# A constant column as second source for a clamp and a normalisation, and a scalar operand for a minimum

## The chip, the core and the metric

The kernel runs on one core of one Trainium2 chip. The metric is the device time of one execution in microseconds (us). The core has five engines that run side by side and wait for one another through semaphores: TensorE (PE, with its weight loads shown apart as PEld), VectorE (DVE), ScalarE (ACT), GpSimd (POOL) and SyncE (SP), which issues all DMAs here. A profiled execution gives the busy time of each engine, every instruction's start and duration, and the clock that TensorE was granted, as a share of full speed.

## The reference

Block attention over 8 batches, 8 heads, 576 positions and head width 64 is followed by a feed-forward layer over the 8 x 576 = 4608 tokens:

```
scores = scale * q @ k.T                     # masked where block_i < block_j, blocks of 64
attn   = exp(scores - rowmax);  attn /= rowsum + 1e-9
x      = heads of (attn @ v), side by side   # 4608 x 512
h      = x @ w_in                            # 512 x 2048
g      = h if h >= 1, 0 if h <= -1, else (h + 1)^2 / 4
out    = g @ w_out                           # 2048 x 512
```

Everything is fp32 in memory.

## The kernel before, in words

TensorE multiplies in a reduced-precision fp32 form (F32R). So an operand that needs full precision is split into a high part, which is the value cast to that form, and a low part, which is the remainder, and a product is three matmuls: high by high, high by low, low by high.

**Attention** goes over 32 pairs (`Pair`): 8 batches by 4 pairs of heads. For each pair, `scores` makes tiles of scores in PSUM for one head (two matmuls, L484 and L487), DVE takes the row maxima (L508), ACT exponentiates and adds up the rows (L513), DVE adds a small constant (L494), takes reciprocals (L495) and multiplies the tile by them (L519). The last 64 query rows of both heads are handled together by `scores_last`: it is 576 columns wide, in two halves, so it has two maxima (L533), the smaller of their negatives is taken (L537), ACT exponentiates (L539), and DVE makes the reciprocal of the sum (L543, L547) and multiplies the 128x576 tile `pr` by it in place (L548). TensorE then transposes the normalised tiles (L561 in batch 0, L559 later), they are copied out, and multiplied with v (L598). Batches 0 and 1 are "plain" (`PLAIN = 2`): the normalised weights and v are used there as plain fp32, without the split. There are 4 pairs in a batch, so 8 of the 32 pairs are plain.

**The weights** are converted once, at the start. `convert` handles a piece of 128x512 words, of which there are 16 of `w_in` and 16 of `w_out`: a DMA brings the words, ACT scales them in two steps (L170, L171), DVE clamps the scaled value between two constants (L172), shifts it (L175) and joins the sign bit to it (L178), POOL adds the low part (L184), ACT casts the high part (L186) and POOL subtracts to get the low part (L188). The high and low parts of `w_in` stay in SBUF (`wih`, `wil`), and those of `w_out` go back to memory (`wo_split`). The words lie in `bits`, a pool of three buffers, so a piece can only be loaded when the piece three before it is finished. L172 and L175 read one operand from SBUF, and L178 reads two.

**The feed-forward layer** goes in 9 chunks of 512 tokens by 16 column blocks of 128. `ffn_in` makes `ph` with twelve matmuls (L777) and the gate from it (ACT L786, DVE L787 and L790, ACT L791, POOL L792), and `ffn_out` multiplies by `w_out` (L801, L806).

**Order.** The loop at the bottom of the kernel walks through the steps of attention, eight a pair. Before step 36 it also draws 12 weight pieces (and two more ahead), after it one feed-forward step for each step of attention, and the remaining pieces as the feed-forward layer needs them. When attention is done, the remaining feed-forward steps follow. The source sets dependencies and priorities; a scheduler then lays out each engine's instructions as one fixed list when the program is built, by its own estimates of how long each takes. An engine runs its list strictly in that order. A changed instruction can therefore change the order of others.

Of the kernel before, what the change touches and what calls it, by code (L numbers as in the profile page):

```python
# [8 lines left out]
F32 = mybir.dt.float32  # L9
F32R = mybir.dt.float32r  # L10
AF = mybir.ActivationFunctionType
ALU = mybir.AluOpType
# [11 lines left out]
def block_attn_then_ffn(  # L24
# [9 lines left out]
    nc = tc.nc  # L34
    B, H, S, D = q.shape
    NT, DM = out.shape
    DF = w_in.shape[1]
    P = 128
# [16 lines left out]
    CW = 512  # L55
    F32_TOP = float.fromhex("0x1.dffffcp-96")
# [7 lines left out]
    const = ctx.enter_context(tc.tile_pool(name="const", bufs=1))  # L64
# [13 lines left out]
    def work_bank(name):  # L78

        banks["n"] += 1  # L80
        if banks["free"] and banks["n"] % 2:
            return ps_o.tile([P, 512], F32, tag="po", name=name)
        return ps_w.tile([P, 512], F32, tag="work", name=name)
# [23 lines left out]
    def last_blocks(t_):  # L107
# [19 lines left out]
        out=msel[:NTL, : NTL * BLK].rearrange("p (t c) -> p t c", c=BLK),  # L127
# [24 lines left out]


    shifted = []

    def wide_tile(dtype, name):
        return conv.tile([P, 2 * CW], dtype, tag="bits", name=name)

    def convert(n, source, hi, lo, done):

        bits = wide_tile(I32, "bits").rearrange("p (n t) -> p n t", t=2)
        if not shifted:
            shifted.append(att1.tile([P, CW], U32, tag="x32", name="shifted"))
        tmp = shifted[0]
        nc.sync.dma_start(bits, source.bitcast(I32).rearrange("p (n t) -> p n t", t=2))
        top, low = bits[:, :, 1].bitcast(F32), bits[:, :, 0]
        words = top.bitcast(U32)


        nc.scalar.mul(top, top, 2.0**-112)  # L170
        nc.scalar.mul(low, low.bitcast(U32), 2.0**-29)  # L171
        nc.vector.tensor_scalar(  # L172
            out=top, in0=top, scalar1=F32_TOP, scalar2=-F32_TOP, op0=ALU.min, op1=ALU.max
        )
        nc.vector.tensor_scalar(  # L175
            out=tmp, in0=words, scalar1=3, scalar2=None, op0=ALU.logical_shift_left
        )
        nc.vector.scalar_tensor_tensor(  # L178
            out=words, in0=words, scalar=0x80000000, in1=tmp,
            op0=ALU.bitwise_and, op1=ALU.bitwise_or,  # L180
        )
        yield
        w32 = bits[:, :, 1]
        nc.gpsimd.tensor_tensor(out=w32, in0=w32, in1=low, op=ALU.add)  # L184
        w32 = w32.bitcast(F32)
        nc.scalar.copy(hi(), w32)  # L186
        yield
        nc.gpsimd.tensor_tensor(out=lo(), in0=w32, in1=hi().bitcast(F32), op=ALU.subtract)  # L188
        if done:
            done()  # L190
# [26 lines left out]
    def prepare_weights():  # L217

        live = []
        for n, piece in enumerate(weight_pieces()):  # L220
            live = [c for c in live + [convert(n, *piece)] if next(c, True) is None]
            yield
        for _ in range(LAG):
            live = [c for c in live if next(c, True) is None]
            yield
# [8 lines left out]
    def as_float32r(src, plain):  # L234

        if plain:
            wide = src.shape[1] > RING - 2 * S
            places = SPARE_WIDE if wide else SPARE
            moved = [places[spare[wide] % len(places)]]
            spare[wide] += 1  # L240
            if src.shape[1] > TCH:
                if "end" not in spare:
                    spare["end"] = att1.tile([P, G0 + P], F32R, tag="pa11", name="pre")[:, :BLK]
                moved.append(spare["end"])
            for i, dst in enumerate(moved):
                n = min(TCH, src.shape[1] - i * TCH)
                nc.sync.dma_start(dst[:, :n].bitcast(F32), src[:, i * TCH : i * TCH + n])
            return moved
        n, moved = src.shape[1], []
        wide = wide_tile(F32R, "prr")  # L250
        nc.sync.dma_start(wide[:, :n].bitcast(F32), src)
        for c0 in range(0, n, TCH):
            moved.append(wide[:, c0 : min(c0 + TCH, n)])
        return moved


    class Pair:
# [264 lines left out]
        def scores_last(self):  # L522

            half = S // 2
            pr = att3.tile([P, S], F32, tag="pr", name="pr")
            nm = small.tile([P, 3], F32, tag="nm", name="nm")
            sm = small.tile([P, 3], F32, tag="sm", name="sm")
            banks = []
            for i in range(2):
                ps = work_bank("ps_s")  # L530
                for j in range(2):
                    self.product(ps[:, :half], j, SM, i * half, half, j == 0, j == 1)
                nc.vector.tensor_reduce(  # L533
                    out=nm[:, i : i + 1], in_=ps[:, :half], axis=AX.X, op=ALU.max, negate=True
                )
                banks.append(ps)
            nc.vector.tensor_tensor(out=nm[:, 2:3], in0=nm[:, 0:1], in1=nm[:, 1:2], op=ALU.min)  # L537
            for i in range(2):
                nc.scalar.activation(  # L539
                    pr[:, i * half : (i + 1) * half], banks[i][:, :half], AF.Exp,  # L540
                    bias=nm[:, 2:3], scale=1.0, accum_out=sm[:, i : i + 1],
                )
            nc.vector.tensor_scalar(  # L543
                out=sm[:, 2:3], in0=sm[:, 0:1], scalar1=sm[:, 1:2], scalar2=EPS,
                op0=ALU.add, op1=ALU.add,
            )
            nc.vector.reciprocal(sm[:, 2:3], sm[:, 2:3])  # L547
            nc.vector.tensor_scalar_mul(pr, pr, sm[:, 2:3])  # L548
            self.pr["last"] = as_float32r(pr, self.plain) if self.hop else [pr]

        def split(self, ps, hi, lo=None):
# [340 lines left out]
```

## Time and profile before

| | us |
|---|---|
| median of 3 runs | 1239.24 (1237.13 to 1243.8) |
| the profiled execution, its time | 1239.06 |
| its span, first to last instruction | 1237.3 |
| PE busy | 1186.6 (96%) |
| DVE busy | 863.8 (70%) |
| ACT busy | 698.5 (56%) |
| POOL busy | 371.8 (30%) |

The time of the profiled execution is 1.8 us more than its span, which is what lies around the first and the last instruction. A row of the groups of instructions reads: line, engine and operation, output and input tile, shape, count, then the busy time of the group and the mean duration of one in ns, then the idle time of the engine just before them and what ended it. A row of the chain of waits reads: start in us, length in us, what held the chain there. A row of a table by stretches gives, for each stretch, its length, the busy time of each engine with its number of instructions, the granted TensorE clock, the busy share of the DMA engines and the memory traffic.

### The profile page before, as it was taken

Reading aid. Unit: us, or ns where it says so; the run is one execution under the profiler, and the core shown is the slowest. Engines: PE = TensorE matmul, PEld = TensorE weight load, DVE = VectorE, ACT = ScalarE, POOL = GpSimd, SP = SyncE. Lnnn points to the kernel's source line nnn. Section 1 sums busy time; section 2 is a strip of 40 time slices with the busy share of each in tenths; the row PEclk is TensorE's granted clock in tenths of the full one; section 3 lists DMA queues with packets and bytes.
Section 4 is the critical chain, followed back from the end, with each engine's and each line's share of the span. In section 5 each row is a group of like instructions: output and inputs, shape, how many; then the busy total and the mean of one; then the engine's idle time right before and its main releaser. Section 6 shows DMA issues by size and latency. Waiting matters only on the chain.

```text
span 1237.3 us, 19822 instructions
## 1 busy us (share of the span) xinstructions
PE 1186.6 (96%) x6280; PEld 993.1 (80%) x6280; DVE 863.8 (70%) x2124; ACT 698.5 (56%) x1731; POOL 371.8 (30%) x366
## 2 busy tenths in 40 slices
PE   4878898999999999999999999999999999999998
PEld 3666677788888888888888888888888888888886
DVE  8888778658777877787777877787778776322322
ACT  5877667546566656665666665666566654222222
POOL 3444546312222222222222222222222222222222
PEclk9988998999999999999999999999999999999999
DMA  5756776778986655565555555565556443333332
GB/s 165 213 176 208 235 247 221 225 202 255 291 270 219 192 162 156 147 198 166 163 159 180 164 160 160 148 196 151 155 149 192 142 135 111 119 102 102 120 103 102
DMA packets 177192, 215.40 MB, mean 174 GB/s; under 512 B 109872, under 2 KB 128304, under 8 KB 176320
## 3 DMA queue, kind: packets, MB, share of 16 engines
q1 hardware_dynamic: 177088, 214.14, 56.1%
q8 instruction: 50, 0.82, 0.3%
q14 instruction: 54, 0.44, 0.1%
HBM read 134.74 MB, written 31.98 MB: 135 GB/s over the span
## 4 chain that ended last, share of the span: by engine, by line
PE 86%; DVE 5%; DMA 4%; ACT 2%; issue 2%; POOL 1%; SPq 0%; ACTq 0%; DVEq 0%; POOLq 0%
PE ph L777 31%; PE po L801 20%; PE po L806 10%; PE ps_av L598 9%; PE ps_s L484 5%; PE ps_s L487 4%; PE ps_t L559 4%; PE ps_qk L403 1%; DMA bits<-in_moe_w_in_dram 1%; DVE bits L172 1%; POOL bits L184 1%; PE ps_t L561 1%; DVE nm L508 1%; DVE bits L178 1%; DVE shifted L175 1%
## 5 line engine op out<-in xcount | busy, mean ns | idle before, releaser
L792 POOL TENSOR_TENSOR gl<-t,gh 128x512 fp32r<-128x512 f32 x144 | 186.5, 1295 | 522.8 <-ACT gh L791 338.2
L801 PE MATMUL po<-wo,gh 128*128 128x512 f32 x1152 | 294.1, 396 | 0.1
L801 PEld LDWEIGHTS po<-wo,gh 128*128 128x128 f32 x1152 | 211.2, 188 | 43.3 <-ACT gh L791 0.6
L777 PE MATMUL ph<-xh,wih 128*128 128x512 f32 x576 | 232.7, 404 | 0.4 <-DVE t L790 0.4
L777 PE MATMUL ph<-xh,wil 128*128 128x512 f32 x576 | 228.1, 396 | 0.0
L777 PE MATMUL ph<-xl,wih 128*128 128x512 f32 x576 | 226.9, 394 | 0.0
L787 DVE SCALAR_TENSOR_TENSOR t<-t 128x512 f32<-128x512 f32 x144 | 101.0, 701 | 161.5 <-ACT t L786 158.6
L786 ACT ACTIVATE t<-ph 128x512 f32<-128x512 f32 x144 | 86.2, 599 | 160.5 <-PE ph L777 160.5
L791 ACT CAST gh<-t 128x512 fp32r<-128x512 f32 x144 | 89.4, 621 | 118.9 <-DVE t L790 118.8
L806 PE MATMUL po<-wo,gl 128*128 128x512 f32 x576 | 155.3, 391 | 0.0
L484 PE MATMUL ps_s<-ka,qa 68*128 68x288 f32 (+4 forms) x384 | 133.8, 363 | 4.9 <-DMA ka<-mrow 4.0
L513 ACT ACTIVATE pr<-ps_s,nm 128x128 f32<-128x128 f32 x192 | 100.4, 525 | 57.5 <-DVE nm L508 56.4
L508 DVE TENSOR_REDUCE nm<-ps_s 128x1 f32<-128x128 f32 (+3 forms) x256 | 118.9, 482 | 16.4 <-PE ps_s L487 15.6
L777 PEld LDWEIGHTS ph<-xh,wil 128*128 128x128 f32 x576 | 109.1, 189 | 24.0
L806 PEld LDWEIGHTS po<-wo,gl 128*128 128x128 f32 x576 | 108.0, 188 | 22.9
L777 PEld LDWEIGHTS ph<-xl,wih 128*128 128x128 f32 x576 | 109.6, 190 | 19.3
L777 PEld LDWEIGHTS ph<-xh,wih 128*128 128x128 f32 x576 | 109.2, 190 | 19.3 <-DVE t L790 0.8
L381 POOL TENSOR_TENSOR vsr<-vn,vsr 64x64 fp32r<-64x64 f32 (+1 forms) x96 | 56.5, 589 | 227.1 <-ACT vsr L380 226.0
L487 PE MATMUL ps_s<-kb,qb 128*128 128x288 f32 (+4 forms) x384 | 120.4, 321 | 0.0
L790 DVE TENSOR_TENSOR t<-ph,t 128x512 f32<-128x512 f32 x144 | 98.7, 685 | 2.0
L559 PEld LDWEIGHTS ps_t<-ident_r,prr 128*128 128x128 f32 x600 | 68.5, 139 | 22.4 <-issue 0.5
L494 DVE TENSOR_SCALAR sm<-sm 128x1 f32<-128x1 f32 x256 | 38.5, 151 | 65.0 <-ACT pr L513 54.8
(115 smaller groups left out, 1879.7 us busy)
## 6 DMA issues: line engine op xcount, KB each, us to landing
wo<-wo_split SPq DMA_DIRECT2D x144, 512.0 KB, 3.4
prr<-pr SPq DMA_DIRECT2D x96, 192.0 KB, 3.0
prr<-pr SPq DMA_DIRECT2D x48, 256.0 KB, 2.8
out_dram<-ob SPq DMA_DIRECT2D x36, 256.0 KB, 2.9
bits<-in_moe_w_in_dram SPq DMA_DIRECT2D x16, 512.0 KB, 4.6
bits<-in_moe_w_out_dram SPq DMA_DIRECT2D x16, 512.0 KB, 4.0
wo_split<-ws SPq DMA_DIRECT2D x16, 512.0 KB, 2.9
qa<-qb SPq DMA_DIRECT2D x63, 128.0 KB, 2.4
```

The lines of the kernel that those rows point to most:

```text
L484: nc.tensor.matmul(ps, qa[:KA, j, c0 : c0 + P], ka[:KA, j, k0 : k0 + n], start=first, stop=False)
L487: nc.tensor.matmul(ps, qb[:, j, c0 : c0 + P], kb[:, j, k0 : k0 + n], start=False, stop=last)
L508: nc.vector.tensor_reduce(out=nm[:, i : i + 1], in_=ps[:, cs], axis=AX.X, op=ALU.max, negate=True)
L513: nc.scalar.activation(raw[:, cs], ps[:, cs], AF.Exp, bias=nm[:, i : i + 1], scale=1.0, accum_out=sm[:, i : i + 1],)
L559: nc.tensor.transpose(out.bitcast(F32R), src, ident_r)
L598: nc.tensor.matmul(ps[:, lo_col:], vt, x, start=first and i == 0 and m == 0, stop=last and i == len(parts) - 1 and m == len(mov) - 1,)
L777: nc.tensor.matmul(ph, w[:, cc, fs], x[:, cc, xs], start=(cc == 0 and i == 0), stop=(cc == NCC - 1 and i == 2),)
L787: nc.vector.scalar_tensor_tensor(out=t_, in0=t_, scalar=1.0, in1=t_, op0=ALU.min, op1=ALU.mult)
L790: nc.vector.tensor_tensor(out=t_, in0=ph, in1=t_, op=ALU.max)
L792: nc.gpsimd.tensor_tensor(out=gl, in0=t_, in1=gh.bitcast(F32), op=ALU.subtract)
L801: nc.tensor.matmul(po[tt], gh[:, ts_], wo[:, w, :], start=(fc == 0 and w == 0), stop=False)
L806: nc.tensor.matmul(po[tt], gl[:, ts_], wo[:, 0, :], start=False, stop=fc == NFC - 1)
```

## The change

There is a new tile `floor` of 128x2, whose first column holds the lower bound of the clamp and whose second holds zeros. Three kinds of DVE instruction are rewritten, all with the same result:

- the clamp of the weights' words (32 instructions, one a piece): a `tensor_scalar` with two immediates becomes a `scalar_tensor_tensor`, whose minimum has an immediate and whose maximum has the first column of `floor`, repeated 512 times, as second source;
- the multiplication of the last block's tile in batches 0 and 1 (8 instructions): a `tensor_scalar` with a scalar column becomes a `scalar_tensor_tensor` that multiplies by the same scalar and then takes the maximum with the zero column, repeated 576 times;
- the minimum of the two negated maxima (32 instructions): a `tensor_tensor` of two columns becomes a `tensor_scalar` with the second column as scalar operand.

```diff
@@ -152,6 +152,9 @@
     shifted = []
+    floor = const.tile([P, 2], F32, tag="floor", name="floor")
+    nc.vector.memset(floor[:, :1], -F32_TOP)
+    nc.vector.memset(floor[:, 1:], 0.0)
@@ -169,8 +172,9 @@
         nc.scalar.mul(top, top, 2.0**-112)
         nc.scalar.mul(low, low.bitcast(U32), 2.0**-29)
-        nc.vector.tensor_scalar(
-            out=top, in0=top, scalar1=F32_TOP, scalar2=-F32_TOP, op0=ALU.min, op1=ALU.max
+        nc.vector.scalar_tensor_tensor(
+            out=top, in0=top, scalar=F32_TOP, in1=floor[:, :1].to_broadcast([P, CW]),
+            op0=ALU.min, op1=ALU.max,
         )
@@ -534,7 +538,9 @@
-            nc.vector.tensor_tensor(out=nm[:, 2:3], in0=nm[:, 0:1], in1=nm[:, 1:2], op=ALU.min)
+            nc.vector.tensor_scalar(
+                out=nm[:, 2:3], in0=nm[:, 0:1], scalar1=nm[:, 1:2], scalar2=None, op0=ALU.min
+            )
@@ -545,7 +551,13 @@
             nc.vector.reciprocal(sm[:, 2:3], sm[:, 2:3])
-            nc.vector.tensor_scalar_mul(pr, pr, sm[:, 2:3])
+            if self.plain:
+                nc.vector.scalar_tensor_tensor(
+                    out=pr, in0=pr, scalar=sm[:, 2:3], in1=floor[:, 1:].to_broadcast([P, S]),
+                    op0=ALU.mult, op1=ALU.max,
+                )
+            else:
+                nc.vector.tensor_scalar_mul(pr, pr, sm[:, 2:3])
```

The lists of all engines also change their order, in the part of the program that converts weights; behind it they are the same as before, apart from the rewritten instructions. Line numbers after the change are 3 to 12 higher: the clamp is L175 there, the shift L179, the joining of the sign L182, the maxima L512 and L537, the minimum L541, the small constant L498, the reciprocals L499 and L553, the scaling of score tiles L523 and the last block's L555.

The first place is DVE's list where the first weight pieces come. Before:

```order
L172 TENSOR_SCALAR bits<-bits 128x512
L175 TENSOR_SCALAR shifted<-bits 128x512
L178 SCALAR_TENSOR_TENSOR bits<-bits,shifted 128x512
L508 TENSOR_REDUCE nm<-ps_s 128x1 x2
L172 TENSOR_SCALAR bits<-bits 128x512
L508 TENSOR_REDUCE nm<-ps_s 128x1
L175 TENSOR_SCALAR shifted<-bits 128x512
L494 TENSOR_SCALAR sm<-sm 128x1
L459 CAST qa<-ps_qk 64x2x64
L494 TENSOR_SCALAR sm<-sm 128x1
L178 SCALAR_TENSOR_TENSOR bits<-bits,shifted 128x512
```

The same place after the change:

```order
L175 SCALAR_TENSOR_TENSOR bits<-bits,floor 128x512
L179 TENSOR_SCALAR shifted<-bits 128x512
L512 TENSOR_REDUCE nm<-ps_s 128x1 x2
L182 SCALAR_TENSOR_TENSOR bits<-bits,shifted 128x512
L498 TENSOR_SCALAR sm<-sm 128x1
L175 SCALAR_TENSOR_TENSOR bits<-bits,floor 128x512
L498 TENSOR_SCALAR sm<-sm 128x1
L512 TENSOR_REDUCE nm<-ps_s 128x1
L499 RECIPROCAL sm<-sm 128x2
L179 TENSOR_SCALAR shifted<-bits 128x512
```

The first two row maxima of the scores now stand ahead of the first piece's last step, and the small sums ahead of the second piece's clamp and shift.

The second place is DVE's list just ahead of the last block's multiplication in the fourth pair, the last of batch 0. Before:

```order
L519 TENSOR_SCALAR pr<-ps_s,sm 128x512
L175 TENSOR_SCALAR shifted<-bits 128x512
L172 TENSOR_SCALAR bits<-bits 128x512
L543 TENSOR_SCALAR sm<-sm 128x1
L178 SCALAR_TENSOR_TENSOR bits<-bits,shifted 128x512
L547 RECIPROCAL sm<-sm 128x1
L494 TENSOR_SCALAR sm<-sm 128x1
L508 TENSOR_REDUCE nm<-ps_s 128x1
L548 TENSOR_SCALAR pr<-pr,sm 128x576
```

After the change:

```order
L175 SCALAR_TENSOR_TENSOR bits<-bits,floor 128x512
L523 TENSOR_SCALAR pr<-ps_s,sm 128x512
L512 TENSOR_REDUCE nm<-ps_s 128x1 x2
L179 TENSOR_SCALAR shifted<-bits 128x512
L549 TENSOR_SCALAR sm<-sm 128x1
L512 TENSOR_REDUCE nm<-ps_s 128x1
L553 RECIPROCAL sm<-sm 128x1
L498 TENSOR_SCALAR sm<-sm 128x1
L182 SCALAR_TENSOR_TENSOR bits<-bits,shifted 128x512
L555 SCALAR_TENSOR_TENSOR pr<-pr,sm,floor 128x576
```

The clamp moved ahead of the scaling of the 128x512 score tile, the joining of the sign moved behind the reciprocal of the last block, and of the clamps one fewer stands ahead of this multiplication than before (13, and 14 before).

## The prediction

> **What bounds the kernel now.** I read the page's strip of slices first, then a table by stretches, then the chain of waits of the first 240 us, then the groups of DVE instructions. The strip and the table:
>
> ```profile
> PE   4878898999999999999999999999999999999998
> DVE  8888778658777877787777877787778776322322
> PEclk9988998999999999999999999999999999999999
> ...
> 20.00:120.00 100.00, 80.61 (x433) 65.33 (x432) 88.52 (x250) 77.97 (x204) 46.51 (x42) 0.91 0.64 194
> 120.00:220.00 100.00, 89.93 (x450) 71.40 (x450) 77.55 (x165) 67.19 (x150) 52.92 (x46) 0.95 0.72 233
> 240.00:1030.00 790.00, 788.86 (x4370) 669.47 (x4370) 611.74 (x1541) 482.35 (x1239) 211.77 (x221) 1.00 0.59 180
> ```
>
> The kernel has two parts. From 240 to 1030 us PE is busy 788.86 of 790 us: nothing that DVE does there can cost more than a little. Before that PE has gaps, and DVE is the fullest engine: 88.5% from 20 to 120 us, 77.6% from 120 to 220. The work of PE is fixed, so the kernel's time moves by what its gaps before 240 us grow or shrink. All 32 clamps and all 8 plain normalisations lie before 240 us, 17 of the clamps before 120 (DVE busy time of line 172 by stretches):
>
> ```profile
> 0.00:120.00 120.00, 13.37 (x17) 0.93 0.64 193
> 120.00:240.00 120.00, 8.29 (x15) 0.96 0.71 227
> ```
>
> **The clamp, 32 times.** The groups of DVE by shape, and for two lines the shortest, median and longest duration in ns:
>
> ```profile
> L178 DVE SCALAR_TENSOR_TENSOR bits<-bits,shifted 128x512 uint32<-128x512 uint32 x32 | 25.9, 810 | 0.5
> L172 DVE TENSOR_SCALAR bits<-bits 128x512 f32<-128x512 f32 x32 | 21.7, 677 | 11.1 <-ACT bits L170 10.5 <-issue 0.5
> ...
> L172 DVE TENSOR_SCALAR bits<-bits x32: 409/430/1657, 11.8 to 217.5; 128x512 f32<-128x512 f32 x32
> ...
> L178 DVE SCALAR_TENSOR_TENSOR bits<-bits,shifted x32: 675/692/1836, 12.7 to 219.1; 128x512 uint32<-128x512 uint32 x32
> ```
>
> The clamp takes 430 ns undisturbed. The new form does not occur with a repeated column, but line 178 is the same operation on the same strided words with a second source in SBUF, and takes 692 ns. I price the new clamp at 692: +262 ns each, 32 x 0.262 = 8.4 us. The lower bound is nothing (a repeated column costs no second stream: 430), the upper the same +262.
>
> Why are the means, 677 and 810, so far above the medians? Instructions of both forms are held while POOL works (start, length):
>
> ```profile
> 63.47 1.66 DVE L172 TENSOR_SCALAR bits<-bits 128x512 f32<-128x512 f32 x1
> ...
> 63.30 1.54 POOL L366 TENSOR_TENSOR ks<-kn,ks 128x576 fp32r<-128x576 f32 x1
> ...
> 136.89 1.84 DVE L178 SCALAR_TENSOR_TENSOR bits<-bits,shifted 128x512 uint32<-128x512 uint32 x1
> ...
> 136.87 1.31 POOL L792 TENSOR_TENSOR gl<-t,gh 128x512 fp32r<-128x512 f32 x1 [2.93 <-DVE shifted L175]
> ```
>
> The clamp at 63.47 ends 0.29 us after POOL's subtraction ended at 64.84; the two-source instruction at 136.89 ends 0.55 us after POOL's at 138.18. Each waits for POOL's instruction to end and then does its work. The holds of the clamp are (677 - 430) x 32 = 7.9 us in all. Since the two-source form is held as well, I leave them where they are, and the change frees nothing.
>
> [...]
>
> **How much of it is on the path.** The chain of waits of the first 240 us gives the clamp 4.0%:
>
> ```profile
> by line: PE ps_av L598 9.3%; PE ph L777 8.0%; issue 8.0%; DMA bits<-in_moe_w_in_dram 6.2%; DVE bits L172 4.0%; POOL bits L184 3.8%; PE ps_t L561 3.8%; DVE nm L508 3.5%; DVE bits L178 2.9%; DVE shifted L175 2.9%; DVE pr L519 2.6%; DMA wo_spl
> ...
> 15.54 1.46 DVE bits L172
> ...
> 217.51 1.08 DVE bits L172
> ```
>
> That is 9.6 of the clamp's 21.7 us, 44%. Counted by pieces, the chain holds 14 clamps between the two shown (and a stub of 0.06 us). 14 x 0.262 = **3.7 us**; 44% of 8.4 gives the same. The other 18 clamps lie beside waits for loads or ahead of work not yet due; what covers them is DVE's idle time, 11.5 us from 20 to 120 and 22.5 us from 120 to 220. If that cover is gone, they cost the remaining 4.7 us. Behind the clamp on DVE stand the shift and the sign step of the same piece and, in the list, row maxima and score scalings, for which ACT and PE's transposes wait; POOL's addition and the release of the buffer come later by the same amount.
>
> **The last block's multiplication, 8 plain pairs.** The groups, and the four that lie on that chain, with what the chain spent in them:
>
> ```profile
> L548 DVE TENSOR_SCALAR pr<-pr,sm x32: 508/521/1384, 28.3 to 1028.0; 128x576 f32<-128x576 f32 x32
> ...
> L354 DVE SCALAR_TENSOR_TENSOR qs<-qn,qs x8: 743/752/1595, 4.5 to 184.0; 128x576 fp32r<-128x576 f32 x8
> ...
> 50.66 0.43 DVE pr L548
> 71.34 1.01 DVE pr L548
> 94.90 0.85 DVE pr L548
> 155.88 1.13 DVE pr L548
> ```
>
> Line 354 is a two-source instruction of the same width from SBUF: 752 ns against 521, so +231 ns, 1.8 us for eight. Four are on the chain: **0.9 us**. Here PE's transposes wait directly. The lower bound is again nothing.
>
> **The minimum, 32 times.** A column by a column becomes a column with a scalar column:
>
> ```profile
> L537 DVE TENSOR_TENSOR nm<-nm x32: 144/159/873, 24.7 to 1026.2; 128x1 f32<-128x1 f32 x32
> ...
> L543 DVE TENSOR_SCALAR sm<-sm x32: 198/214/216, 27.4 to 1027.5; 128x1 f32<-128x1 f32 x32
> ```
>
> Line 543 has a scalar column and a second operation, and takes 55 ns longer; with one operation I expect 0 to 55 ns. For the eight before 240 us that is at most 0.4 us, and I take **0.2**; for the 24 later ones PE's full occupancy covers it. ACT's exponentials of the last block wait behind it. The two small memsets of the new tile stand at the very start, where DVE waits for the first loads: 0.
>
> **Moved instructions.** The lists change order only before the stage in which PE is full. The amount of work ahead of each landmark (each last-block multiplication, each gate) stays the same to one or two short instructions, for instance one clamp fewer ahead of the fourth multiplication; I take 0, with the two sides as rivals.
>
> **Sum**: 3.7 + 0.9 + 0.2 = 4.8 us on the profiled execution's 1239.06 us: **1243.9**. That execution lies 0.2 us below the median of the runs, 1239.24, which gives 1244.0. I predict **1244**, which is 0.4% slower. The bounds are 0 and everything on the path, 8.4 + 1.8 + 0.4 = 10.6 us: 1239 and 1250.
>
> **The rivals.** I call faster or slower what differs by over 0.5%, 6.2 us, about what a measurement of this kernel can tell: below 1233.0 or above 1245.4.
>
> *DVE is the bound before 120 us, and the clock follows.* The place is PE's gap before the last block's transposes:
>
> ```profile
> 90.00:95.00 5.00, 1.44 (x8) 0.69 (x7) 4.17 (x15) 3.79 (x12) 2.94 (x3) 0.91 0.33 65
> 95.00:100.00 5.00, 4.11 (x17) 3.51 (x18) 3.91 (x12) 4.22 (x10) 3.25 (x3) 0.50 0.82 286
> ...
> 92.61 0.33 PE L487 MATMUL ps_s<-kb,qb 128*128 128x384 f32 x1
> 95.89 0.44 PE L561 MATMUL ps_t<-ident_r,pr 128*128 128x128 f32 x1 [2.94 <-DVE sm L494]
> ...
> 94.83 0.92 DVE L548 TENSOR_SCALAR pr<-pr,sm 128x576 f32<-128x576 f32 x1
> ```
>
> PE is idle for 2.95 us until the multiplication ends at 95.75, and in the next five microseconds it has half its clock: 4.11 busy us at 0.50 are 2.1 us lost. If the whole 10.6 us comes on the path and one more such half-speed stretch with it, the time is 1239.1 + 10.6 + 2.1 = **1252**. It decides when DVE's 11.5 idle us from 20 to 120 cannot be used, so that its share there goes above some 93%. For it: 88.5% is already high, and the price of a gap is paid twice. Against: 56% of the clamp's time is off the chain now.
>
> [...]
>
> *DVE's idle time takes it.* As before, with the minimum's and some of the multiplications' 1 us: **1240**. For it: 11.5 and 22.5 us idle. Against: most of the idle time waits for an input and isn't free where it is needed.
>
> [...] If a repeated column isn't held, the 14 clamps on the chain gain what they now spend above 430 ns there, about 9.6 - 14 x 0.43 = 3.6 us, and pay 3.7; if the engine keeps the fast form, nothing changes. Either way about **1239**, so not slower. The held rows of line 178 speak against the first, its 692 ns against the second.
>
> *The new order closes gaps.* PE's transposes of the plain batches wait for DVE's normalisation:
>
> ```profile
> L561 PE MATMUL ps_t<-ident_r,pr 128*128 128x128 f32 (+1 forms) x100 | 21.1, 335 | 18.8 <-DVE pr L519 9.7 <-DVE sm L494 6.9 <-ACT qb L429 2.2
> ```
>
> If normalisations come ahead of conversions often enough to halve these 18.8 us, and two half-speed stretches of 2.1 us go with them, the kernel gains 9.4 + 4.2 and pays 4.8: 1239.1 - 8.8 = **1230**. One clamp fewer ahead of the fourth multiplication speaks for it; that the other landmarks have the same work ahead as before speaks against.
>
> **Chances.** The forecast (1241 to 1247) 0.41, all on the path 0.25, hidden 0.17, freed or no stream 0.06, gaps closed 0.11. A quarter of the forecast's own range lies above 1245.4 and a little of the gap case within the bound: slower 0.25 + 0.13 = 0.38, faster 0.11, within 0.5% the remaining 0.51. For eight times in ten I take **1236 to 1252**: it leaves out most of the gap case below, and the worse part of the full-path case above.
>
> **What would show it.** The new clamp's median near 692 ns and its longest still above 1.5 us, the plain multiplication's near 752, the minimum's between 159 and 214; DVE's busy time from 20 to 120 us up by 3 to 6 us; PE's busy time from 240 to 1030 as full as now, begun about 5 us later. A clamp that stays at 430 ns, or one of 692 that POOL never holds, would prove the pricing wrong; a start of PE's full stretch that moves by nothing, or by over 10 us, the share on the path; and half-clock stretches that come or go, the zero for the order.

## The result and the profile after

The changed kernel takes **1246.09 us** (median of 11 runs, 1243.36 to 1249.88), the kernel before 1239.24 (11 runs). The ratio is 1.0054 [1.0036, 1.0071]: 0.5% slower, +6.85 us. The forecast was 1244. The profiled execution after took 1245.28 us, its span 1243.5 (before 1239.06 and 1237.3).

One sentence of the description of the kernel has to be corrected: not everything is fp32 in memory. The two weight matrices arrive as 64-bit floats; a piece of `bits` holds pairs of 32-bit words, and the conversion (scaling, clamp, shift, sign, addition) makes 32-bit floats of them.

The strip of slices and the table by stretches of the changed kernel (columns as in the table of before: PE, PEld, DVE, ACT, POOL, granted clock, DMA share, GB/s):

```profile
PE   4888898999999999999999999999999999999998
DVE  8999779658777877787778777787778775222322
PEclk9998998999999999999999999999999999999999
...
20.00:120.00 100.00, 82.55 (x432) 65.98 (x433) 94.21 (x254) 77.73 (x205) 49.51 (x43) 0.93 0.68 205
120.00:220.00 100.00, 89.78 (x438) 71.22 (x436) 80.82 (x159) 63.13 (x145) 55.25 (x47) 0.93 0.70 225
240.00:1030.00 790.00, 787.94 (x4361) 668.00 (x4361) 611.89 (x1537) 480.94 (x1234) 212.09 (x221) 1.00 0.59 179
```

DVE is busier by 5.7 us from 20 to 120 us and by 3.3 from 120 to 220, and PE is as full as before from 240 on. What looks odd is PE from 20 to 120: it is busier too, 82.55 against 80.61. The path got longer and PE's gaps got shorter at the same time, so more than one thing happened.

The durations of the three rewritten kinds (shortest, median and longest in ns, then first and last start):

```profile
L175 DVE SCALAR_TENSOR_TENSOR bits<-bits,floor x32: 671/692/1717, 11.7 to 221.6; 128x512 f32<-128x512 f32 x32
L555 DVE SCALAR_TENSOR_TENSOR pr<-pr,sm,floor x8: 805/815/1827, 28.8 to 240.0; 128x576 f32<-128x576 f32 x8
L541 DVE TENSOR_SCALAR nm<-nm x32: 200/214/216, 26.3 to 1029.8; 128x1 f32<-128x1 f32 x32
```

The clamp with its repeated column takes as long as the sign step with its full second source took before: 692 ns, as priced. The multiplication takes 815, not 752, and the minimum 214 against 159.

The conversion's groups by shape (busy us, mean ns of one), first the shift before, then clamp, sign step and shift after:

```profile
L175 DVE TENSOR_SCALAR shifted<-bits 128x512 uint32<-128x512 uint32 x32 | 16.4, 513 | 0.5
```

```profile
L175 DVE SCALAR_TENSOR_TENSOR bits<-bits,floor 128x512 f32<-128x512 f32 x32 | 27.1, 847 | 11.6 <-ACT bits L173 10.1 <-issue 1.3
L182 DVE SCALAR_TENSOR_TENSOR bits<-bits,shifted 128x512 uint32<-128x512 uint32 x32 | 26.7, 834 | 0.1
L179 DVE TENSOR_SCALAR shifted<-bits 128x512 uint32<-128x512 uint32 x32 | 21.6, 676 | 0.1
```

The clamp's group grew by 5.4 us (27.1 - 21.7), not by 8.4: its holds are now (847 - 692) x 32 = 5.0 us instead of 7.9. The shift behind it, which nobody rewrote, grew by 5.2 us: it is held more. By the timeline 10 of its 32 take 0.99 to 1.52 us, each of them beside an instruction of POOL; before it was 3, of 1.26 to 1.39. In all DVE is busy 877.0 us against 863.8, +13.2. POOL's subtractions into `wil` are longer too, before and after:

```profile
L188 POOL TENSOR_TENSOR wil<-bits,wih x16: 1290/1308/1703, 15.4 to 204.3; 128x512 fp32r<-128x512 f32 x16
```

```profile
L192 POOL TENSOR_TENSOR wil<-bits,wih x16: 1290/1534/1809, 18.0 to 206.9; 128x512 fp32r<-128x512 f32 x16
```

Their median rose by 226 ns. Whether the repeated column or the new order did this to the shift and to POOL is answered with e2 below. One held clamp in the timeline after (start, length):

```profile
29.19 1.81 POOL L192 TENSOR_TENSOR wil<-bits,wih 128x512 fp32r<-128x512 f32 x1
...
29.84 1.72 DVE L175 SCALAR_TENSOR_TENSOR bits<-bits,floor 128x512 f32<-128x512 f32 x1
```

POOL's instruction ends at 31.00 and the clamp 0.56 us later. So the clamp with the repeated column is held as well, here for 1.72 us against its median of 692 ns. All 10 clamps that take over 0.75 us lie beside an instruction of POOL; but 15 of the 22 shorter ones overlap one too, at least in part, so not every such meeting is a hold.

Where the time is lost along the run is read from two groups: the 24 last-block multiplications behind the conversion, first and last start, and the last of the gate's instructions. Before, then after:

```profile
L548 DVE TENSOR_SCALAR pr<-pr,sm x24: 519/521/523, 274.3 to 1028.0; 128x576 f32<-128x576 f32 x24
L787 DVE SCALAR_TENSOR_TENSOR t<-t x129: 681/692/695, 268.4 to 1227.1; 128x512 f32<-128x512 f32 x129
```

```profile
L560 DVE TENSOR_SCALAR pr<-pr,sm x24: 519/520/522, 276.5 to 1031.6; 128x576 f32<-128x576 f32 x24
L799 DVE SCALAR_TENSOR_TENSOR t<-t x129: 681/692/694, 270.5 to 1233.2; 128x512 f32<-128x512 f32 x129
```

Up to the ninth multiplication, where everything that the prediction costed has happened, only 2.2 us are lost. Another 1.4 us go between there and 1030 us, and **2.5 us in the last 200 us**, where almost only feed-forward is left and no instruction or place in a list differs from before.

### The profile page after: what moved, and what is told of

It reads as the page before. It is cut to its first block, busy times and chain, and to the rows that moved or that the text cites. A ratio compares the mean times of both kernels' runs of the same rounds, so it can differ in the third digit from the quotient of the medians.

```text
span 1243.5 us, 19828 instructions
## 1 busy us (share of the span) xinstructions
PE 1194.3 (96%) x6280; PEld 995.0 (80%) x6280; DVE 877.0 (71%) x2126; ACT 697.2 (56%) x1731; POOL 378.9 (30%) x366
## 4 chain that ended last, share of the span: by engine, by line
PE 84%; DVE 6%; DMA 4%; ACT 2%; issue 2%; POOL 1%; SPq 0%; ACTq 0%; DVEq 0%; POOLq 0%
PE ph L789 30%; PE po L813 20%; PE po L818 10%; PE ps_av L610 9%; PE ps_s L488 5%; PE ps_s L491 4%; PE ps_t L571 4%; DMA bits<-in_moe_w_in_dram 2%; PE ps_qk L407 1%; DVE bits L175 1%; DVE bits L182 1%; POOL bits L188 1%; DVE shifted L179 1%; DVE pr L523 1%; DMA wo_split<-ws 1%
## 5 line engine op out<-in xcount | busy, mean ns | idle before, releaser
L512 DVE TENSOR_REDUCE nm<-ps_s 128x1 f32<-128x128 f32 (+3 forms) x256 | 118.5, 481 | 10.2 <-PE ps_s L491 9.2
L488 PEld LDWEIGHTS ps_s<-ka,qa 68*128 68x128 f32 x384 | 74.3, 193 | 12.4 <-DVE shifted L179 3.6
```

Source lines behind the costliest of these rows:

```text
L488: nc.tensor.matmul(ps, qa[:KA, j, c0 : c0 + P], ka[:KA, j, k0 : k0 + n], start=first, stop=False)
L512: nc.vector.tensor_reduce(out=nm[:, i : i + 1], in_=ps[:, cs], axis=AX.X, op=ALU.max, negate=True)
```

## The experiments

Two things change together: the instructions, and through them the order of all lists. They can be held apart. In most of these kernels the lists are laid out for one version; then, in the finished lists, single instructions are exchanged for those of the other. Order, waits and buffers stay those of the first version. Except where a wider one is named, all have the tile `floor` and its two memsets. Each ratio stands against the kernel before, run on the same chip in the same set; its median there was 1239.53, 1240.03 and 1239.22 us for the three sets (e1 to e4, e5 to e8, e9 to e12).

### Order and instructions apart (e1, e2)

e1 has the order of before and all new instructions. `SWAP` holds the instructions of each kind, `low` and `zero` are the two columns of `floor`, `cut` repeats a column, and `swap` puts each new instruction in the place of the old one (the lines that fill `SWAP`, and `cut` and `swap` themselves, are left out here and below):

```diff
...
+    low, zero = (h.ins.outs[0] for h in SWAP["floor"])
+    new = {}
+    for h in SWAP["clamp"]:
+        i = h.ins
+        new[i.name] = copy.replace(
+            i, ins=(i.ins[0], i.ins[1], cut(low, [[0, 512]])), is_scalar_tensor_tensor=True
+        )
+    for b, h in SWAP["norm"]:
+        if b < 2:
+            i = h.ins
+            new[i.name] = copy.replace(
+                i, ins=(i.ins[0], i.ins[1], cut(zero, [[0, 576]])), op1=_mybir.AluOpType.max,
+                is_scalar_tensor_tensor=True,
+            )
+    for b, h in SWAP["min"]:
+        i = h.ins
+        new[i.name] = copy.replace(
+            SWAP["clamp"][0].ins, name=i.name, debug=i.debug, sync_info=i.sync_info, ins=i.ins,
+            outs=i.outs, op0=_mybir.AluOpType.min, op1=_mybir.AluOpType.bypass,
+        )
+    swap(nc, new)
```

> The lists of all engines stand in the order of the kernel before; only the 32 clamps, 8 plain multiplications and 32 minima are the new instructions (put into the finished lists). Theory (the longer instructions cost the time, about 44% of what is added is on the path): +4 to +7 us, and a profile with clamps of 692 ns. Rival, the new order: 0 to +1 us. Rival, DVE is the bound: +10 us or more.

Measured: 1251.5 us, 1.0099 [1.0082, 1.0115].

e2 is the reverse: laid out for the changed kernel, and then the old instructions put back (`tensor_scalar` for clamp and multiplication, `tensor_tensor` for the minimum).

```diff
...
+    for h in SWAP["clamp"]:
+        i = h.ins
+        new[i.name] = copy.replace(
+            i, ins=(i.ins[0], i.ins[1], copy.replace(i.ins[1], value=-i.ins[1].value)),
+            is_scalar_tensor_tensor=False,
+        )
+    for b, h in SWAP["norm"]:
+        i = h.ins
+        new[i.name] = copy.replace(
+            i, ins=(i.ins[0], i.ins[1]), op1=_mybir.AluOpType.bypass, is_scalar_tensor_tensor=False
+        )
...
```

> The lists of all engines stand in the order of the changed kernel; the 72 rewritten instructions are put back to the old ones. Theory: 0, within 1.5 us. Rival, the new order: +5 to +7 us. If order and length each do a part, this and the run with the old order add up to the change.

Measured: 1237.29 us, 0.9983 [0.9972, 0.9993]: faster than before. So the new order is no neutral thing. With the new instructions it is worth 1.0054 - 1.0099 = -0.45%, 5.6 us. The rival "the new order closes gaps" had named the place, PE's transposes of the plain batches. That group of PE up to 276 us, after, in e2 and in e1 (behind the second bar: idle time ahead of it, and what ended that):

```profile
L573 PE MATMUL ps_t<-ident_r,pr 128*128 128x128 f32 (+1 forms) x100 | 21.4, 336 | 14.0 <-DVE sm L498 6.9 <-DVE pr L523 5.4 <-ACT bits L174 1.6
```

```profile
L591 PE MATMUL ps_t<-ident_r,pr 128*128 128x128 f32 (+1 forms) x100 | 21.3, 335 | 13.9 <-DVE sm L516 7.3 <-DVE pr L541 4.5 <-ACT pb L582 2.0
```

```profile
L583 PE MATMUL ps_t<-ident_r,pr 128*128 128x128 f32 (+1 forms) x100 | 23.0, 360 | 18.5 <-DVE pr L539 10.0 <-DVE sm L514 5.7 <-ACT ws L206 2.7
```

Before it was 18.8, of which 9.7 for the scaling of the score tiles. In the new order it is 14.0 and 13.9, with the new instructions or the old; in the old order it stays at 18.5. The same holds for all kernels here: 13.2 to 14.0 in the four with the new order, 16.6 to 20.5 in the others. The part that waits for the scalings is about halved. This is not the whole account of the order: ahead of the first matmuls of `ph`, PE's idle time up to 276 us rises from 0.4 to 3.7 us after the change and 3.1 in e2, so the 5.6 us are not added up place by place. Nor is it shown which moves did it. Counted in the lists, among the steps of the conversion, 20 of 58 row maxima and 25 of 56 small sums have fewer of these steps ahead of them than before (6 and 8 have more), but of the 56 scalings 16 have fewer and 12 more.

e1 and e2 also tell who lengthened the shift and POOL's subtractions. Clamp, shift and subtraction in e2 (new order, old instructions), then in e1 (old order, new instructions):

```profile
L193 DVE TENSOR_SCALAR bits<-bits 128x512 f32<-128x512 f32 x32 | 18.5, 577 | 10.9 <-ACT bits L191 9.2 <-issue 1.6
...
L197 DVE TENSOR_SCALAR shifted<-bits 128x512 uint32<-128x512 uint32 x32 | 19.8, 619 | 0.1
...
L210 POOL TENSOR_TENSOR wil<-bits,wih x16: 1290/1443/1756, 18.0 to 201.8; 128x512 fp32r<-128x512 f32 x16
```

```profile
L192 DVE SCALAR_TENSOR_TENSOR bits<-bits,floor 128x512 f32<-128x512 f32 x32 | 29.8, 932 | 11.2 <-ACT bits L190 10.3 <-issue 0.9
...
L195 DVE TENSOR_SCALAR shifted<-bits 128x512 uint32<-128x512 uint32 x32 | 18.2, 568 | 0.5
...
L208 POOL TENSOR_TENSOR wil<-bits,wih x16: 1289/1318/1852, 15.5 to 214.8; 128x512 fp32r<-128x512 f32 x16
```

In e2, where no instruction reads a repeated column, the shift already takes 619 ns (513 before) and the subtraction 1443 (1308 before). In e1, where the clamps do, they are at 568 and 1318. So most of both comes from the order, which decides what meets POOL. With the order held, from e2 to the changed kernel, the clamps grow by 27.1 - 18.5 = 8.6 us, about as priced, and the shifts by 1.8.

### One part at a time, in the old order (e3, e5, e6), the clamp doubled (e4) and removed (e8)

e3 exchanges the clamps alone. Against e1:

```diff
     for h in SWAP["clamp"]:
...
-    for b, h in SWAP["norm"]:
...
-    for b, h in SWAP["min"]:
...
```

> Old order, only the 32 clamps are new: 32 x 0.262 = 8.4 us more on DVE. Theory: 14 on the path, +3.7 us. [...] Rival, DVE is the bound: +8.4 us.

Measured: 1247.2 us, 1.0061 [1.0045, 1.0077].

e4 exchanges the clamps, and also gives the shift a second source, the column of zeros, with which it is joined by "or". Against e3:

```diff
...
+    for h in SWAP["shift"]:
+        i = h.ins
+        nought = copy.replace(cut(zero, [[0, 512]]), dtype=i.ins[0].dtype)
+        new[i.name] = copy.replace(
+            i, ins=(i.ins[0], copy.replace(i.ins[1], dtype=i.ins[0].dtype), nought),
+            op1=_mybir.AluOpType.bitwise_or,
+            is_scalar_tensor_tensor=True,
+        )
```

> Old order, the clamps are new and the 32 shifts get a repeated column of zeros as second source too, so that the dose is doubled: about 17 us more on DVE in the same places. Theory, a constant share on the path: twice the clamp alone, +7 to +8 us. Rival, DVE becomes the bound once its idle time is used: more than twice, +10 to +17 us. Rival, a slack that is used up first: clamp alone near 0, this one +4 or more.

Measured: 1255.49 us, 1.0122 [1.0107, 1.0138]. The shift with its second source:

```profile
L195 DVE SCALAR_TENSOR_TENSOR shifted<-bits,floor x32: 667/693/1673, 12.6 to 230.9; 128x512 uint32<-128x512 uint32 x32
```

e5 exchanges the eight multiplications alone. Against e1:

```diff
-    for h in SWAP["clamp"]:
...
     for b, h in SWAP["norm"]:
...
-    for b, h in SWAP["min"]:
...
```

> Old order, only the 8 plain multiplications are new (815 ns by the profile of the changed kernel, 521 before: 8 x 0.294 = 2.4 us). Forecast's share (4 of 8 on the path): +1.2 us. Rival, all on the path, as the clamp's 7.6 of 8.4 us now say: +2.4 us. Rival, the clock's half-speed stretches answer to such a delay: over +4 us.

Measured: 1246.66 us, 1.006 [1.0042, 1.0077].

e6 exchanges the 32 minima alone. Against e1:

```diff
-    for h in SWAP["clamp"]:
...
-    for b, h in SWAP["norm"]:
...
     for b, h in SWAP["min"]:
...
```

> Old order, only the 32 minima are new (214 ns for 159: 32 x 0.055 = 1.8 us). Forecast: +0.2 us, the 24 late ones covered by PE. Rival, the late ones count too: +1.8 us. The sum of the three parts should give the 12.0 us of all new instructions in the old order; the clamp gave 7.6, so 4.4 are left for this and the plain multiplications.

Measured: 1244.43 us, 1.0044 [1.0027, 1.006]. That cannot be the minimum: 32 x 0.055 = 1.8 us in all, most of it under a full PE, and yet the kernel is 5.4 us slower (0.0044 x 1240). Every single part alone comes out 0.4 to 0.6% slower, as if a constant came with it.

e8 keeps the old form, but clamps one word of 512; the words that it leaves out are not bounded.

```diff
...
+    for h in SWAP["clamp"]:
+        i = h.ins
+        one = cut(i.outs[0], [[2, 1]])
+        new[i.name] = copy.replace(i, ins=(one, *i.ins[1:]), outs=(one,))
```

> Old order, but each clamp does 1 column instead of 512, so the other 511 words of a row are not bounded: 430 ns become about 160, 32 x 0.27 = 8.6 us less on DVE. The share of 44%: -4 us. A share of 90%, as the longer clamp showed: -8 us. Rival, the idle time that the longer clamp used up is not there to be gained: 0 to -2 us.

Measured: 1238.11 us, 0.9989 [0.9976, 1.0002]. The 32 clamps now take 149 ns each:

```profile
L192 DVE TENSOR_SCALAR bits<-bits x32: 134/149/155, 11.8 to 210.8; 128x1 f32<-128x1 f32 x32
```

Nearly all the clamp's work is gone (its group falls to 4.7 us), and the time is that of before. Here too something adds what the missing clamp saves.

### Long late minima (e7)

The 24 minima behind the conversion become reductions that read the two columns 256 times:

```diff
...
+    for b, h in SWAP["min"]:
+        if b >= 2:
+            i = h.ins
+            r = SWAP["reduce"].ins
+            new[i.name] = copy.replace(
+                r, name=i.name, debug=i.debug, sync_info=i.sync_info,
+                ins=(cut(i.ins[0], [[0, 256], [1, 2]]),), outs=i.outs,
+                op=_mybir.AluOpType.min, axis=_mybir.AxisListType.XY, negate=False,
+            )
```

> Old order and old instructions, but in the 24 pairs that are not plain the minimum is a reduction that reads its two columns 256 times (about 680 ns for 159, as the maxima over 512 columns take; the result is the same): 24 x 0.52 = 12.5 us more on DVE in the stage in which PE is full. Forecast (PE's full occupancy covers it): 0 to +1 us. Rival (the late minima are on the path): +6 us or more.

Measured: 1244.64 us, 1.0055 [1.0035, 1.0076]. The reductions, and the stretch in which they lie:

```profile
L558 DVE TENSOR_REDUCE nm<-nm x24: 685/686/689, 271.7 to 1028.8; 128x1 f32<-128x512 f32 x24
...
240.00:1030.00 790.00, 787.39 (x4350) 666.67 (x4350) 622.15 (x1534) 479.86 (x1234) 211.86 (x221) 1.00 0.59 180
```

DVE has 10.4 us more there than before, 622.15 against 611.74, and PE is as full as ever.

### The tile alone (e9)

What e1 to e8 have in common is the tile. e9 is the kernel before with the tile and its memsets; no instruction uses it, and the lists are those of before:

```diff
     shifted = []
+    floor = const.tile([P, 2], F32, tag="floor", name="floor")
+    nc.vector.memset(floor[:, :1], -F32_TOP)
+    nc.vector.memset(floor[:, 1:], 0.0)
```

> The kernel before with the new tile and its two memsets alone; no instruction is rewritten and all lists keep their order. The tile takes 8 bytes a partition and moves every later tile by 32 bytes. The forecast had this at 0. New theory from the profiles (the matmuls of the last 200 us take 394 to 396 ns for 390 to 391 in every variant that has the tile): +3.5 to +4.5 us, of which 2.5 lie after 1030 us. Rival (those profiles differ by chance): 0.

Measured: 1245.62 us, **1.0046** [1.0033, 1.0059]. A tile of 8 bytes a partition that nobody reads, with its two memsets, costs 5.7 us (0.0046 x 1239.2; 4.1 to 7.3 by the interval), almost as much as the whole change. The two groups that date the loss:

```profile
L551 DVE TENSOR_SCALAR pr<-pr,sm x24: 519/521/523, 276.4 to 1031.9; 128x576 f32<-128x576 f32 x24
L790 DVE SCALAR_TENSOR_TENSOR t<-t x129: 682/692/694, 270.5 to 1233.5; 128x512 f32<-128x512 f32 x129
```

It loses 2.1 us by the ninth multiplication, 1.8 more by the 32nd, and 2.5 in the last 200 us. Not at the start, where the memsets are. The sign steps up to 212 us, before and in e9:

```profile
L178 DVE SCALAR_TENSOR_TENSOR bits<-bits,shifted x30: 675/692/1836, 12.7 to 210.5; 128x512 uint32<-128x512 uint32 x30
```

```profile
L181 DVE SCALAR_TENSOR_TENSOR bits<-bits,shifted x30: 673/693/1841, 12.7 to 210.6; 128x512 uint32<-128x512 uint32 x30
```

The 30th starts 0.1 us later. Behind it one stretch of PE differs in clock:

```profile
219.00:226.00 7.00, 6.55 (x31) 5.07 (x32) 5.20 (x17) 3.95 (x13) 4.51 (x5) 1.00 0.65 189
```

```profile
219.00:226.00 7.00, 5.84 (x23) 4.83 (x24) 3.89 (x12) 3.88 (x11) 3.91 (x3) 0.76 0.45 132
```

Before, the clock is full there; in this execution of e9 it is 0.76. e7 is the same program as e9 up to its first long minimum at 271.7 us, and it doesn't show this. The same stretch in e7, and the start of its ninth multiplication:

```profile
219.00:226.00 7.00, 7.00 (x34) 5.33 (x32) 4.63 (x15) 4.06 (x13) 4.53 (x5) 1.00 0.69 208
...
L570 DVE TENSOR_SCALAR pr<-pr,sm x24: 520/521/523, 274.0 to 1031.1; 128x576 f32<-128x576 f32 x24
```

So the 2.1 us up to the ninth multiplication are not shown to be the tile's. The other two parts come back: the ten kernels with the narrow tile (the changed one and e1 to e9) lose 0.7 to 1.9 us between the ninth multiplication and the 32nd (e7, whose longer minima lie there, 3.4) and 2.0 to 2.6 behind it. In e9 these two parts make 4.3 us.

In the last 200 us the matmuls themselves are longer. PE's groups from 1045 to 1225 us before and in e9 (busy us, mean ns):

```profile
L801 PE MATMUL po<-wo,gh 128*128 128x512 f32 x262 | 65.0, 390 | 0.0
L777 PE MATMUL ph<-xh,wih 128*128 128x512 f32 x131 | 51.2, 391 | 0.0
L777 PE MATMUL ph<-xh,wil 128*128 128x512 f32 x130 | 50.8, 391 | 0.0
L777 PE MATMUL ph<-xl,wih 128*128 128x512 f32 x130 | 50.6, 389 | 0.0
```

```profile
L804 PE MATMUL po<-wo,gh 128*128 128x512 f32 x256 | 64.5, 394 | 0.0
L780 PE MATMUL ph<-xh,wil 128*128 128x512 f32 x129 | 51.1, 396 | 0.0
L780 PE MATMUL ph<-xl,wih 128*128 128x512 f32 x128 | 50.3, 393 | 0.0
L780 PE MATMUL ph<-xh,wih 128*128 128x512 f32 x128 | 50.1, 391 | 0.0
```

Three of the five large groups take 4 to 5 ns longer, 1%; `ph<-xh,wih` and the fifth, `po<-wo,gl`, stay at 391. PE is not idle ahead of any of them. The three add up to 256 x 4 + 129 x 5 + 128 x 4 ns = 2.2 us in this window, nearly all of the 2.5 us.

### The tile 64 bytes wide (e10, e11, e12)

The tile changes where others lie. In the built programs it stands at the end of its pool, and every tile of the later pools begins 32 bytes further on, among them `t`, `gh`, `gl`, `wo`, `bits`, `pr` and `vs`, which had begun at multiples of 64. `xh`, `xl`, `wih` and `wil` lie ahead of it and don't move. With 16 columns, of which two are used, the later tiles move by 64.

```diff
-    floor = const.tile([P, 2], F32, tag="floor", name="floor")
+    floor = const.tile([P, 16], F32, tag="floor", name="floor")[:, :2]
```

e10 is the changed kernel with that tile:

> The changed kernel with the new tile made 64 bytes wide (16 columns, of which two are used), so that the later tiles lie at multiples of 64 bytes again, as in the kernel before. New theory: 3.5 to 4.5 us less than the changed kernel, so +2 to +3.5 us over the kernel before. Rival (the place of the tiles does nothing): +6.8 us, as the changed kernel.

Measured: 1245.0 us, 1.0043 [1.0031, 1.0055]. Its groups of PE from 1045 to 1225 us:

```profile
L813 PE MATMUL po<-wo,gh 128*128 128x512 f32 x256 | 63.8, 391 | 0.0
L789 PE MATMUL ph<-xh,wih 128*128 128x512 f32 x128 | 50.6, 395 | 0.0
L789 PE MATMUL ph<-xh,wil 128*128 128x512 f32 x128 | 50.3, 393 | 0.0
L789 PE MATMUL ph<-xl,wih 128*128 128x512 f32 x128 | 49.8, 389 | 0.0
```

Two of the longer groups are back, to 391 and 389 ns, and `ph<-xh,wil` is at 393. But `ph<-xh,wih`, which the narrow tile left alone, now takes 395, though neither of its operands moved. Against before these make 1.0 us (256 x 1 + 128 x 4 + 128 x 2 ns).

e11 is e2 (new order, old instructions) with it:

> The new order with the old instructions, and the tile 64 bytes wide. With the narrow tile it was 2.1 us faster than the kernel before. New theory: the order is worth 6 us and the tile took 4 of them back: -5 to -6.5 us. Rival (the place does nothing): -2.1 us.

Measured: **1236.76 us**, 0.9976 [0.9966, 0.9985]. This beats both kernels, the one before by 0.24%. Its two groups:

```profile
L578 DVE TENSOR_SCALAR pr<-pr,sm x24: 519/521/523, 270.7 to 1024.8; 128x576 f32<-128x576 f32 x24
L817 DVE SCALAR_TENSOR_TENSOR t<-t x129: 680/692/696, 264.7 to 1225.0; 128x512 f32<-128x512 f32 x129
```

e12 is e1 (old order, new instructions) with it:

> The old order with all new instructions, and the tile 64 bytes wide. With the narrow tile it was 12.0 us slower than the kernel before. New theory: +7.5 to +8.5 us, the length of the instructions alone. Rival (the place does nothing): +12 us.

Measured: 1251.12 us, 1.0095 [1.0082, 1.0108].

In the profiles the width shows every time in the last stage. From the last of the 24 multiplications to the last gate it is 199.1 us before, 201.1 to 201.7 in all ten kernels with the narrow tile (the changed one and e1 to e9), and 200.0 to 200.2 in the three with the wide one. So in the last stage the width of a tile that is otherwise the same is worth about 1.5 us: that is shown. In the total the three pairs differ by 0.11, 0.07 and 0.04% in favour of the wide tile, each with an uncertainty of 0.15% or more: 1.5 us would be 0.12% and doesn't stand out. From the ninth multiplication to the 32nd the width does nothing: there each wide kernel takes as long as its partner to 0.3 us. So most of the tile's cost stays, and e11 doesn't win by its tile, but by its order.

What exactly costs the rest is **open**: the places of other tiles (with a move by 64 bytes the last stage still takes 1 us more), chance in the first 270 us, or something that shifts with two more instructions at the head of DVE's list. How a place acts is open too. The addresses come from the built programs, and a matmul's own operands are not the whole answer: those of L777 didn't move, and two of its three groups got longer. A tile that moves no other, and memsets without a tile, weren't tried.

## Why the prediction was nearly right, and its steps wrong

The forecast was 2.1 us too low, a small error made of three large ones. That they nearly cancel is luck. The forecast's mechanism, longer DVE instructions of which a share is on the path, is one of the three. Along one way through the experiments, before to changed:

| step | kernels | ratio difference | us | forecast |
|---|---|---|---|---|
| tile and memsets | before to e9 | +0.46% | +5.7 | 0 |
| new order | e9 to e2 | -0.63% | -7.8 | 0 |
| longer instructions | e2 to after | +0.71% | +8.8 | +4.8 |

Along the other way (e9 to e1, then to after) the instructions cost 6.6 us and the order gives 5.6. Differences of two ratios are uncertain by about 0.2%, 2 to 3 us, so the two ways agree.

**"The two small memsets of the new tile ... 0" failed.** Their own time is hidden, as said (the 30th sign step is 0.1 us late), but a new tile is not only its memsets. It moves others, and the prediction put no term and no rival there. Of the 5.7 us, 4.3 are dated to the stages in which PE is full, where the prediction expected next to nothing.

**"I take 0" for the moved instructions failed.** The working compared amounts of work ahead of landmarks and found them alike. They are alike, and still the order is worth 5.6 to 7.8 us; so what matters lies inside the stretches, in which instruction stands ahead of which, and the lists shown with the change have it: row maxima and small sums ahead of the conversion's steps. The rival that closes gaps named what happened, though not all of it. It hoped to halve the 18.8 us ahead of the transposes; 14.0 are left, and other waits grew. Its half-speed stretches became fewer in the median execution: the mean granted clock is 0.987 in e9 and 0.9915 in e2, 0.985 in e1 and 0.988 after. All this came along with the forecast's costs and not instead of them.

**The clamp's price held, its share on the path less so.** 692 ns, still held, was right: the longest, 1717 ns, refutes that a repeated column isn't held, and the median that the clamp keeps the form of 430 ns. But DVE got more than the priced 10.6 us: 12.5 in the new order (e2 to after) and 13.9 in the old (e9 to e1). One reading of the holds was loose. After POOL's instruction ended, the two held instructions took 0.29 and 0.55 us more, less than their undisturbed 0.43 and 0.69; so, if the profile's ends on POOL are exact, they did not wait for that end with all of their work. And of the two only L178 reads two operands from SBUF; the clamp of before reads one and was held all the same, for 1.66 us. How much of added DVE time reaches the end can now be read over several doses, each against its partner that differs in nothing else, with the DVE busy time of each profile:

| pair | DVE busy us | change | time us | share |
|---|---|---|---|---|
| e9 to e8, clamp almost gone | 864.7, 851.6 | -13.1 | -7.1 | 54% |
| e9 to e3, clamp | 864.7, 874.5 | +9.8 | +1.9 | 19% |
| e9 to e5, multiplication | 864.7, 869.1 | +4.4 | +1.7 | 39% |
| e9 to e1, all three | 864.7, 878.6 | +13.9 | +6.6 | 47% |
| e9 to e4, clamp and shift | 864.7, 882.8 | +18.1 | +9.4 | 52% |
| e2 to after, new order | 864.5, 877.0 | +12.5 | +8.8 | 70% |
| e11 to e10, new order | 864.4, 876.9 | +12.5 | +8.3 | 66% |
| e9 to e7, late minima | 864.7, 877.4 | +12.7 | +1.1 | 9% |

With times uncertain by 2 to 3 us, the old order is consistent with the forecast's 44% from the chain of waits; e3 alone lies lower, and no single row settles it. The two rows in the new order are higher, two thirds. But all six rows of the old order stand on the one median of e9: with the 4.3 us that are dated for the tile in place of 5.7, e1 would have 8.0 us or 57%. That the new order lets more of the work through is therefore not shown. So the term of the sum that was mis-sized is the instructions', 4.8 forecast and 6.6 to 8.8 measured, partly by the price and partly by the share.

**The multiplication** was priced at 752 from a two-source instruction; it takes 815. Since it has a scalar column too, the 63 ns are like the 55 that a scalar column adds to the minimum. For eight that is 0.5 us, too small to see in the time.

**The minimum** (e9 to e6, -0.02%) costs nothing that can be measured, and e7 shows why: about 12.5 us of longer late minima cost 1.1 us, not distinguishable from nothing in the total; between the ninth and the 32nd multiplication e7 takes 1.6 us longer than e9 (757.1 and 755.5). The full PE covers nearly all late DVE work, as the prediction said.

**DVE as the bound, with the clock.** DVE went to 94.2% from 20 to 120 us, beyond the 93% that this rival named, yet the time didn't go to 1252, with the order's gain against it. In the old order e1 took 1251.5, but with 5.7 of its us from the tile, and DVE was busy only 88.1% from 20 to 120 us there. So that share doesn't tell the two apart. The price of a half-speed stretch seems too high as well: from one execution to the next of the same kernel (141 runs, each kernel around its own mean), 1 us more of lost clock, reckoned as the span times what the mean granted clock lacks, goes with 0.26 us more of span. That is a correlation; no run changed the clock alone.

Of the signs named at the end, DVE's busy time (+5.7 of 3 to 6), the durations of clamp and minimum and the full PE came out. "Begun about 5 us later" didn't: 2.2 us. And half-clock stretches moved, the sign against the zero for the order: the granted clock rose from 0.91 to 0.93 from 20 to 120 us and fell from 0.95 to 0.93 from 120 to 220.

## What to carry to other kernels

An edit that changes an instruction also changes lists and places, and these can weigh as much as its duration (7.8 and 5.7 us here, beside 8.8): before a small gain or loss is put down to the instruction, run the new order with the old instructions and the new tile with nothing that uses it. When lists are compared, look at which waited-for instruction now stands ahead of which filler, not at how much work lies ahead of a landmark. Where a neighbour got longer too, the same run tells whether the order did it. A repeated column as second source was no cheaper here than a full one, 692 ns each.

## What the runs showed of the hardware

- A tile of 8 bytes a partition that nobody reads, with its memsets, costs 5.7 us of 1239 (4.1 to 7.3). In the last stage three groups of matmuls take 393 to 396 ns instead of 389 to 391, two of them with operands that didn't move, and the stage takes 2.5 us more; with a tile of 64 bytes it is 1.0, and another group, with unmoved operands, takes 395.
- A repeated column as second source takes as long as a full one: 692 ns for the clamp of 128x512 and 693 for the shift, against 692 for the sign step with a full one; beside a POOL instruction the clamp takes up to 1717 ns. POOL's subtractions grow from a median of 1308 to 1534, but to 1443 already in the new order with no repeated column.
- A scalar column instead of a plain second column adds 55 ns to the minimum of 128x1 (159 and 214). The 128x576 multiplication with a scalar column takes 815 ns, and another line's two-source instruction with an immediate 752.
